# Gated mix of a feature-map linear attention and a GeGLU network: the attention state accumulated transposed, with v as the stationary operand, and turned by DMA

## The chip, the cores and the metric

The kernel runs on one core of one Trainium2 chip. A time is in device microseconds (us) of one execution, and the times that are compared are medians of several runs. The kernel before takes 303.22 us (three runs, 303.22 to 305.41). The profile is of one execution; its span, 301.2 us, is a little shorter than the time of that run (302.93 us), because it does not hold everything that the time holds.

The engines are named as in the profile: PE multiplies matrices and has a part PEld that loads the stationary operand; DVE works elementwise and reduces; ACT applies functions and copies; POOL is a third elementwise engine; SP issues most of the DMA transfers. PE's results go to PSUM, which the kernel uses as eight banks of 512 float32 per partition.

## What is computed

One token block of 2048 rows and 640 columns, `x`, goes through two branches. Branch A is linear attention with 32 heads of 20 columns; branch B is a gated network of width 1728. A gate per row mixes them. Cut to what matters:

```python
qkv = (x @ wqkv).reshape(B, S, 3, H, Dh).transpose(2, 0, 3, 1, 4)   # H = 32, Dh = 20
pq = einsum("bhsd,hdf->bhsf", q, w_phi)                  # and pk from k
phi_q = concat([softmax(pq), softmax(-pq)])              # over the 20 features of a head
phi_k = concat([softmax(pk), softmax(-pk)])
kv = einsum("bhsf,bhsd->bhfd", phi_k, v)                 # the state: summed over all rows
z  = einsum("bhsf->bhf", phi_k)
o  = einsum("bhqf,bhfd->bhqd", phi_q, kv) / (einsum("bhqf,bhf->bhq", phi_q, z)[..., None] + 1e-6)
a  = o.reshape(B, S, D) @ wo
b  = (gelu(x @ w_gate) * (x @ w_up)) @ w_down
g  = sigmoid((x * gate_w).sum(-1, keepdims=True))
out = g * a + (1 - g) * b
```

The state `kv` with `z` as one more column is needed whole before the first row of `o` can be computed.

## The kernel before

The 2048 rows are 16 tiles of 128. `wk2` and `wq2` are the key and query weights with `w_phi` multiplied in; the kernel makes them itself, in ten *folds* (five for k, five for q, one for each 128 rows of the weights). `xT` is x with its columns on the partitions; block 0 (tiles 0 to 3) is turned on PE, and blocks 1 to 3 come turned by DMA. The loads that the change touches, in the order of SP's queue:

```python
        wload(self.wkT, D, "wkT")      # transposing DMA of the key weights, for the k folds
        xblock(1)                      # transposing DMA: xT of tiles 4 to 7
        wload(self.wqT, 0, "wqT")
        xblock(2)
        xblock(3)
        ...                            # then the weights of branch B and wo
```

The first stage in program order. `vs` and `ve` are v of tiles 0 to 3; `f(kt, which, banks, engine)` is a fold of six matmuls with 640 columns in all, copied out of PSUM by DVE ("d") or ACT ("a"):

```python
        f = self.fold
        f(0, "k", (6, 7), "d")
        f(1, "k", (0, 1), "a")
        self.v_early(4, 2)             # v of tile 4: 5 matmuls of 512 columns, 5 of 128; copied out by ACT
        f(2, "k", (4, 5), "d")
        f(3, "k", (6, 7), "d")
        self.v_early(5, 0)
        f(4, "k", (4, 5), "d")
        self.k_early(0, 2)             # pk of tile 0: 5 matmuls of 384, 5 of 257; ACT takes exp twice (Ek), then gcol
        f(0, "q", (6, 7), "d")
        f(1, "q", (4, 5), "d")
        self.k_early(1, 0)
        f(2, "q", (6, 7), "d")
        f(3, "q", (4, 5), "d")
        self.k_norm(0)                 # softmax sums and division of Ek on DVE
        self.k_early(2, 2)
        f(4, "q", (6, 7), "a")
        self.k_norm(1)
        self.k_early(3, 0)
        self.pq(0, 1, 1)               # exp(pq), exp(-pq) of 4 tiles x 128 features: 5 matmuls of 512, bank 6 + n % 2
        self.pq(0, 0, 0)
        self.pq(0, 3, 3)
        self.gram(0)
        self.k_norm(2)
        self.pq(0, 2, 2)
        self.k_norm(3)
        n = 4
        g = 1
        for t in range(4, NT):
            if t < 6:
                self.k_early(t, 1)
            else:
                self.vk(t)             # v and pk of one tile: 15 matmuls, 1281 columns x 5
            self.k_norm(t)
            m = 4 + ((t - 3) * (len(order) - 4) + 11) // 12
            while n < m:               # one or two pq for each tile, the grams before the last of them
                ...
```

The gram of a tile adds its part to the state. The keys' features, 128 at a time, are the stationary operand, and v with a column of ones for each head (`vaug`, 21 columns a head) streams past. Only the heads that share a chunk of 128 features are streamed; twelve matmuls, 1512 columns in all, fill banks 3, 4 and 5:

```python
        return {
            3: [full(0, 0), full(0, 1), full(0, 3), (1, 2, 12, 14)],
            4: [full(1, 0), full(1, 1), full(1, 3), (1, 2, 15, 17)],
            5: [full(0, 4), full(1, 4), full(0, 2), (1, 2, 18, 19)],
        }
        ...
                    self.bank(b)[:, c:c + n], self.Ek[:, se, s, i * P:(i + 1) * P], self.vaug[:, sv, h0:h1 + 1, :],
```

After the last tile `kv_evac` multiplies the state by a mask that keeps each head's own block and writes it to `KV` in bfloat16, twelve operations of DVE. `num(t)` then has `KV` streamed past exp(pq): twelve matmuls of 1584 columns, followed by DVE, POOL and a transposing DMA.

Branch B, `ffn`, is interleaved with the end of it. `gateup(b, c)` is ten matmuls of 512 columns, one ACT and one DVE operation (five matmuls for the narrow chunk 13); `down(t)` multiplies by `w_down` and `wo` (38 matmuls of 320 columns):

```python
            if b == 0:
                order = [0, 1, 13] + list(range(2, 13))
                at = {5: 0, 8: 1, 11: 2}          # after which gateup num(0), num(1), num(2) follow
            ...
                if b == 0:
                    if idx == 0:
                        self.gram(14)
                    if idx == 3:
                        self.gram(15)
                        self.kv_evac()
                        self.gates()
                if idx in at:
                    self.num(at[idx])
```

Of the kernel before, what the change touches and what calls it, by code (L numbers as in the profile page):

```python
# [3 lines left out]
P = 128  # L4
# [99 lines left out]
class _Kernel:  # L104
# [99 lines left out]
    def loads(self):  # L204
# [23 lines left out]
        def xblock(b):  # L228
            sc.dma("sp", lambda e: e.dma_start_transpose(
                self.xT[:, :, b * self.BT:(b + 1) * self.BT], self.x[b * self.BT:(b + 1) * self.BT, :]),  # L230
                writes=[("xT", t) for t in range(b * 4, b * 4 + 4)])
        wload(self.wkT, D, "wkT")
        xblock(1)
        wload(self.wqT, 0, "wqT")
        xblock(2)
        xblock(3)
# [133 lines left out]
                start=(kt == 0 and col == 0), stop=(kt == self.KD - 1), skip_group_check=True),  # L370
                reads=[("xT", t), ("wv", kt)], writes=[("ps", bk)], signal=(kt == self.KD - 1))

    def k_step(self, t, kt):
        sc = self.sc
        for c0, n, bk, col in ((640, 384, 2 * t, 128), (1024, 257, 2 * t + 1, 0)):
            sc.op("pe", lambda e, c0=c0, n=n, bk=bk, col=col: e.matmul(
                self.bank(bk)[:, col:col + n], self.xT[:, kt, t * P:(t + 1) * P], self.w3[:, kt, c0:c0 + n],
                start=(kt == 0), stop=(kt == self.KD - 1)),
                reads=[("xT", t), ("wk2", kt), "wgate"], writes=[("ps", bk)], signal=(kt == self.KD - 1))

    def v_first_evac(self, ts, ek, tail):
        sv, nt = ts[0], len(ts)
        h0, nh = (24, 8) if tail else (0, 24)
# [62 lines left out]
            sc.op("dve", lambda e, v=v, r=r: e.tensor_tensor(v, v, r, ALU.mult),  # L446
                  reads=[("Rk", se)], writes=[("Ek", se, s)])

    def gram_regions(self):
        lo = self.HLO  # L450
        full = lambda s, i: (s, i, lo[i], self.HHI[i])
        return {
            3: [full(0, 0), full(0, 1), full(0, 3), (1, 2, 12, 14)],
            4: [full(1, 0), full(1, 1), full(1, 3), (1, 2, 15, 17)],
            5: [full(0, 4), full(1, 4), full(0, 2), (1, 2, 18, 19)],
        }

    def gram(self, t):
        sc = self.sc
        se, sv = t % self.NSE, t % self.NSV  # L460
        for b, regs in self.gram_regions().items():
            c = 0
            for r, (s, i, h0, h1) in enumerate(regs):
                n = (h1 - h0 + 1) * self.DA
                sc.op("pe", lambda e, s=s, i=i, h0=h0, h1=h1, c=c, n=n, b=b, r=r: e.matmul(  # L465
                    self.bank(b)[:, c:c + n], self.Ek[:, se, s, i * P:(i + 1) * P], self.vaug[:, sv, h0:h1 + 1, :],
                    start=(t == 0 and r == 0), stop=(t == self.NT - 1 and r == len(regs) - 1)),
                    reads=[("Ek", se, s), ("vaug", sv), ("vmain", sv), ("vone", sv)], writes=[("ps", b)],
                    signal=(r == len(regs) - 1))
                c += n  # L470

    def kv_evac(self):
        sc = self.sc
        for b, regs in self.gram_regions().items():
            c = 0
            for (s, i, h0, h1) in regs:
                nh = h1 - h0 + 1
                j0 = h0 - self.HLO[i]
                dst = self.KV[:, i, s, j0 * self.DB:(j0 + nh) * self.DB].rearrange(
                    "p (h c) -> p h c", c=self.DB)[:, :, 0:self.DA]  # L480
                src = self.bank(b)[:, c:c + nh * self.DA].rearrange("p (h c) -> p h c", c=self.DA)
                m = self.mask[:, i, j0:j0 + nh].unsqueeze(2).to_broadcast([P, nh, self.DA])
                sc.op("dve", lambda e, dst=dst, src=src, m=m: e.tensor_tensor(dst, src, m, ALU.mult),
                      reads=[("ps", b), ("mask", i), ("KVd", i, s)], writes=[("KV", i, s, h0)])
                c += nh * self.DA

    def pq(self, b, i, n):
        sc = self.sc
# [22 lines left out]
    def attention_state(self):  # L511
        NT = self.NT
        order = [(b, i) for b in range(self.NB) for i in range(self.KD)]
        sc = self.sc
        sc.op("dve", lambda e: e.memset(self.zero[:, :], 0.0), writes=["zero"])
        sc.op("dve", lambda e: e.memset(self.one[:, :], 1.0), writes=["one"])

        def warm(n):
            for i in range(n):
                sc.op("pe", lambda e: e.matmul(self.bank(0), self.zero[:, 0:P], self.zero[:, :], start=True, stop=True),  # L520
                      reads=["zero"], writes=[("ps", 0)])
        vs, ve, xt = self.v_step, self.v_first_evac, self.x_transpose
# [24 lines left out]
        ks = self.k_step  # L547
        f = self.fold
        f(0, "k", (6, 7), "d")
        f(1, "k", (0, 1), "a")  # L550
        self.v_early(4, 2)
        f(2, "k", (4, 5), "d")
        f(3, "k", (6, 7), "d")
        self.v_early(5, 0)
        f(4, "k", (4, 5), "d")
        self.k_early(0, 2)
        f(0, "q", (6, 7), "d")
        f(1, "q", (4, 5), "d")
        self.k_early(1, 0)
        f(2, "q", (6, 7), "d")  # L560
        f(3, "q", (4, 5), "d")
        self.k_norm(0)
        self.k_early(2, 2)
        f(4, "q", (6, 7), "a")
        self.k_norm(1)
        self.k_early(3, 0)
        self.pq(0, 1, 1)
        self.pq(0, 0, 0)
        self.pq(0, 3, 3)
# [4 lines that stand above are left out]
        n = 4  # L574
        g = 1
        for t in range(4, NT):
            if t < 6:
                self.k_early(t, 1)
            else:
                self.vk(t)  # L580
            self.k_norm(t)
            m = 4 + ((t - 3) * (len(order) - 4) + 11) // 12
            while n < m:
                if n == m - 1:
                    for g in range(g, t - 2 if t < 8 else t - 1):
# [36 lines left out]
    def num(self, t):  # L622
# [5 lines left out]
        kvk = {(i, s): [] for i in range(5) for s in (0, 1)}  # L628
        for regs in self.gram_regions().values():
            for (s, i, h0, h1) in regs:  # L630
                kvk[(i, s)].append(("KV", i, s, h0))
        for hf in (0, 1):
            for s in (0, 1):
                bk = NBK + 2 * hf + s
                for r, (i, h0, h1) in enumerate(parts[hf]):
                    n = (h1 - h0 + 1) * DB
                    o0 = (h0 - 16 * hf) * DB
                    k0 = (h0 - self.HLO[i]) * DB
                    sc.op("pe", lambda e, s=s, i=i, n=n, o0=o0, k0=k0, bk=bk, r=r: e.matmul(  # L639
                        self.bank(bk)[:, o0:o0 + n], self.Eq[:, s, i, t * P:(t + 1) * P],  # L640
                        self.KV[:, i, s, k0:k0 + n], start=(r == 0), stop=(r == 2), skip_group_check=True),
                        reads=[("Eq", t // 4, s, i), ("KVd", i, s)] + kvk[(i, s)], writes=[("ps", bk)],
                        signal=(r == 2))
        sl = t % 2
        N = self.ps[:, NBK * 512:(NBK + 4) * 512].rearrange("p (f s c) -> p f s c", s=2, c=512)[:, :, :, 0:16 * DB]
# [76 lines left out]
    def ffn(self):  # L722
# [4 lines left out]
        for b in range(self.NB):  # L727
            if b == 0:
                order = [0, 1, 13] + list(range(2, 13))
                at = {5: 0, 8: 1, 11: 2}  # L730
            else:
                order = list(range(14))
                at = {2: 4 * b + 1, 6: 4 * b + 2, 10: 4 * b + 3}
            for idx, c in enumerate(order):
                if b == 0 and c == 13:
                    self.gateup(b, c, (2,))
                else:
                    self.gateup(b, c, pairs[self.pn % 2])
                    self.pn += 1
# [4 lines that stand above are left out]
                        self.gram(15)  # L744
                        self.kv_evac()
                        self.gates()
                if idx in at:
                    self.num(at[idx])
            for t in range(4):
# [48 lines left out]
```

The softmax here doesn't subtract the row's maximum and nothing guards it: scores larger than these inputs give would overflow.

## Time and profile before

The stages of the one execution, read from the trace in order of time (us from the start of the span), with the busy time of PE, DVE and ACT in it:

| stretch | what runs | PE | DVE | ACT |
|---|---|---|---|---|
| 0 to 10 | loads, turning of block 0, first v | 8.71 | 1.30 | 2.58 |
| 10 to 30 | last v of tiles 0 to 3, folds, first pk, first pq | 18.26 | 15.59 | 12.80 |
| 30 to 60 | tile by tile: v, pk, gram, pq | 29.76 | 27.46 | 20.31 |
| 60 to 301 | rest of that loop, then branch B with the nums | 237.35 | 117.03 | 67.77 |

A busy time of PE counts each matmul from its start to its modelled end, and neighbours overlap, so a stretch in which PE is 98% busy can still have gaps between the starts of its matmuls. What PE waited for is read from the idle entries of its groups and from the chain of work that ended last, and the length of a piece of work from the start of one group to the start of the next.

### The profile page before, as it was taken

Reading aid. Unit: us, or ns where it says so; the run is one execution under the profiler, and the core shown is the slowest. Engines: PE = TensorE matmul, PEld = TensorE weight load, DVE = VectorE, ACT = ScalarE, POOL = GpSimd, SP = SyncE. Lnnn points to the kernel's source line nnn. Section 1 sums busy time; section 2 is a strip of 40 time slices with the busy share of each in tenths; the row PEclk is TensorE's granted clock in tenths of the full one; section 3 lists DMA queues with packets and bytes.
Section 4 is the critical chain, followed back from the end, with each engine's and each line's share of the span. In section 5 each row is a group of like instructions: output and inputs, shape, how many; then the busy total and the mean of one; then the engine's idle time right before and its main releaser. Section 6 shows DMA issues by size and latency. Waiting matters only on the chain.

```text
span 301.2 us, 4951 instructions
## 1 busy us (share of the span) xinstructions
PE 294.1 (98%) x1973; PEld 173.9 (58%) x1999; DVE 161.4 (54%) x317; ACT 103.5 (34%) x182; POOL 29.0 (10%) x58
## 2 busy tenths in 40 slices
PE   8998999999999999999999999999999999999996
PEld 4665656555554555776454577655457765445773
DVE  1469999768685877214467700445770045567000
ACT  3358767576773222112222211222221122222112
POOL 7000000000000022011011100101110010111000
PEclk9999999999999999999999999999999999999999
DMA  7999980000000011110111010011101011110101
GB/s 221 248 214 337 372 285 0 0 2 0 2 0 0 2 22 24 46 44 25 43 25 22 0 46 22 27 41 23 24 0 44 24 33 32 25 22 0 46 22 44
DMA packets 35474, 18.11 MB, mean 60 GB/s; under 512 B 27579, under 2 KB 35196, under 8 KB 35452
## 3 DMA queue, kind: packets, MB, share of 16 engines
q1 hardware_dynamic: 34800, 17.78, 21.8%
q8 instruction: 15, 0.25, 0.4%
q10 hardware_dynamic: 652, 0.03, 0.2%
q14 instruction: 7, 0.06, 0.1%
HBM read 8.96 MB, written 2.62 MB: 38 GB/s over the span
## 4 chain that ended last, share of the span: by engine, by line
PE 92%; SPq 2%; DMA 2%; ACT 1%; issue 1%; DVE 0%; DVEq 0%; ACTq 0%
PE ps L602 36%; PE ps L684 20%; PE ps L359 12%; PE ps L690 7%; PE ps L491 7%; PE ps L639 4%; PE ps L465 4%; DMA xT<-in_A_x_dram 2%; PE ps L612 1%; SPq L226 1%; SPq L216 1%; PE ps L339 1%; ACT Eq L497 1%; ACT Ek L426 0%; DVE w_49 L352 0%
## 5 line engine op out<-in xcount | busy, mean ns | idle before, releaser
L602 PE MATMUL ps<-xT,wu_sb 128*128 128x512 bf16 x253 | 64.2, 379 | 0.8 <-ACT Eq L497 0.2
L684 PE MATMUL ps<-wd_sb,hT 128*128 128x320 bf16 (+2 forms) x447 | 63.5, 299 | 0.1
L602 PE MATMUL ps<-xT,wg_sb 128*128 128x512 bf16 x252 | 63.0, 379 | 0.2
L605 ACT ACTIVATE gl<-ps 128x512 bf16<-128x512 f32 x52 | 31.0, 597 | 83.3 <-PE ps L602 74.2
L607 DVE TENSOR_TENSOR hT<-ps,gl 128x512 bf16<-128x512 f32 x52 | 35.7, 688 | 42.9 <-PE ps L602 42.9
L684 PEld LDWEIGHTS ps<-wd_sb,hT 128*128 128x128 bf16 x448 | 43.1, 98 | 18.2 <-DVE hT L607 0.4
L602 PEld LDWEIGHTS ps<-xT,wu_sb 128*128 128x128 bf16 x260 | 25.4, 98 | 31.1 <-issue 0.7
L359 PE MATMUL ps<-w_49,xT 128*128 128x512 bf16 (+3 forms) x226 | 40.7, 327 | 1.1 <-DMA xT<-in_A_x_dram 0.6
L602 PEld LDWEIGHTS ps<-xT,wg_sb 128*128 128x128 bf16 x260 | 24.9, 98 | 26.9
L668 POOL TENSOR_TENSOR Og<-O_57,O_58 128x640 bf16<-128x640 bf16 x16 | 22.3, 1394 | 167.9 <-DVE O_58 L666 167.9
L700 ACT ACTIVATE outsb<-ps,Gm 128x640 bf16<-128x640 f32 (+2 forms) x17 | 13.0, 762 | 74.1 <-PE ps L690 74.1
L359 PEld LDWEIGHTS ps<-w_49,xT 128*128 128x128 bf16 x230 | 21.7, 97 | 19.7 <-DVE w_49 L352 0.7
L655 DVE RECIPROCAL RH<-ps 128x32 f32<-128x32 f32 x16 | 5.7, 358 | 43.9 <-PE ps L639 42.8
L437 DVE TENSOR_REDUCE Dk<-Ek 128x64 f32<-128x1280 bf16 x16 | 23.7, 1482 | 8.9 <-ACT gcol L429 8.9
L446 DVE TENSOR_TENSOR Ek<-Ek,Dk 128x640 bf16<-128x640 bf16 x32 | 25.0, 822 | 0.6
L690 PE MATMUL ps<-wo_sb,goT 128*128 128x320 bf16 (+2 forms) x160 | 24.5, 299 | 0.0
L491 PE MATMUL ps<-xT,wq_50 128*128 128x512 bf16 x94 | 23.4, 378 | 1.1 <-ACT wq_50 L354 0.7
L497 ACT ACTIVATE Eq<-ps 128x512 bf16<-128x512 f32 x40 | 21.8, 603 | 5.7 <-PE ps L491 5.6
L426 ACT ACTIVATE Ek<-ps 128x640 bf16<-128x640 f32 x32 | 20.8, 706 | 3.4 <-PE ps L359 3.4
L690 PEld LDWEIGHTS ps<-wo_sb,goT 128*128 128x128 bf16 x160 | 15.5, 98 | 6.3
L639 PEld LDWEIGHTS ps<-KV,Eq 128*128 128x128 bf16 x192 | 12.0, 98 | 3.1
L491 PEld LDWEIGHTS ps<-xT,wq_50 128*128 128x128 bf16 x100 | 8.6, 97 | 8.8 <-ACT wq_50 L354 0.7
(66 smaller groups left out, 175.9 us busy)
## 6 DMA issues: line engine op xcount, KB each, us to landing
out_dram<-outsb SPq DMA_DIRECT2D x15, 160.0 KB, 1.8
wd_sb<-in_B_w_down_dram SPq DMA_DIRECT2D x1, 2080.0 KB, 13.5
wg_sb<-in_B_w_gate_dram SPq DMA_DIRECT2D x1, 1120.0 KB, 5.8
wu_sb<-in_B_w_up_dram SPq DMA_DIRECT2D x1, 1120.0 KB, 8.2
wg_sb<-in_B_w_gate_dram SPq DMA_DIRECT2D x1, 960.0 KB, 9.6
wu_sb<-in_B_w_up_dram SPq DMA_DIRECT2D x1, 960.0 KB, 10.4
w_49<-in_A_wqkv_dram SPq DMA_DIRECT2D x5, 160.0 KB, 4.0
wo_sb<-in_A_wo_dram SPq DMA_DIRECT2D x1, 800.0 KB, 10.2
```

The source lines that it names most:

```text
L359: sc.op("pe", lambda e, kt=kt: e.matmul(self.bank(bank)[:, bcol:bcol + n], self.xT[:, kt, t * P:(t + 1) * P], self.w3[:, kt, c0:c0 + n], s ...
L437: sc.op("dve", lambda e: e.tensor_reduce(self.Dk[:, se, 0, :].rearrange("p (s h) -> p s h", h=H), self.Ek[:, se, :, :].rearrange("p s (h d ...
L446: sc.op("dve", lambda e, v=v, r=r: e.tensor_tensor(v, v, r, ALU.mult), reads=[("Rk", se)], writes=[("Ek", se, s)])
L491: sc.op("pe", lambda e, kt=kt: e.matmul(self.bank(bank), self.wq2[:, kt, i * P:(i + 1) * P], self.xT[:, kt, b * self.BT:(b + 1) * self.BT] ...
L497: sc.op("act", lambda e, s=s, scale=scale: e.activation(self.Eq[:, s, i, b * self.BT:(b + 1) * self.BT], self.bank(bank), AF.Exp, scale=sc ...
L602: sc.op("pe", lambda e, kt=kt, w=w, bk=bk: e.matmul(self.bank(bk), w[:, kt, c * P:(c + 1) * P], xs(kt), start=(kt == 0), stop=(kt == self. ...
L605: sc.op("act", lambda e: e.activation(self.gl[:, slot, :], self.bank(banks[0]), AF.Gelu_apprx_tanh), reads=[("ps", banks[0])], writes=[("g ...
L607: sc.op("dve", lambda e: e.tensor_tensor(self.hT[:, c, :], self.bank(banks[1]), self.gl[:, slot, :], ALU.mult), reads=[("ps", banks[1]), ( ...
L639: sc.op("pe", lambda e, s=s, i=i, n=n, o0=o0, k0=k0, bk=bk, r=r: e.matmul(self.bank(bk)[:, o0:o0 + n], self.Eq[:, s, i, t * P:(t + 1) * P] ...
L668: sc.op("pool", lambda e: e.tensor_tensor(self.Og[:, sl, :], self.O1[:, sl, :], self.O2[:, sl, :], ALU.add), reads=[("O", 0, sl), ("O", 1, ...
L684: sc.op("pe", lambda e: e.matmul(self.bank(bk, w), self.hT[:, c, tt * P:(tt + 1) * P], self.wd_sb[:, c, w0:w0 + w], start=(c == 0), stop=F ...
L690: sc.op("pe", lambda e: e.matmul(self.bank(bk, w), self.goT[:, gs, k, :], self.wo_sb[:, k, w0:w0 + w], start=False, stop=(k == self.KD - 1 ...
```

## The change

Four things are changed.

1. *The gram has v stationary and the keys stream.* Six groups of six heads (the last has two). For a group the stationary operand is 128 columns of `vaug` (six heads are 126), and the streamed one is the group's 120 features of both signs, 240 columns; the last group has 80. It makes the state transposed: v on the partitions, features along the free axis. Six matmuls, 1280 columns, instead of twelve and 1512.
2. *The state is turned by DMA.* `kv_evac` copies the three banks into two slots of `Ek` that are free by then (three copies on DVE, one on ACT), and two transposing DMAs turn them into two other slots. Ten masking operations on DVE, now a step of their own (`kv_mask`) after the gateup at position 6, write `KV`. The first three nums move from after positions 5, 8 and 11 to after 8, 11 and 13.
3. *v of tiles 4 to 7 runs early, in between the k folds*, two of them ahead of the first fold; the loop's tiles 6 and 7 then need only pk, and the pq are spread so that tiles 4 to 7 have two each. The banks of the folds change, and the last q fold is copied by DVE instead of ACT.
4. *The second block of x is loaded ahead of the key weights*, so that v of tiles 4 and 5 can start before the key weights are there.

The diff, cut to its core (an unused function is removed as well):

```diff
+        xblock(1)
         wload(self.wkT, D, "wkT")
-        xblock(1)
         wload(self.wqT, 0, "wqT")
@@ gram
-    def gram_regions(self): ...
+    def gram_groups(self):
+        fe = 6 * self.DH
+        for g in range(6):
+            lo = min(6 * g * self.DA, self.H * self.DA - P)
+            yield g, 3 + g % 2 if g < 4 else 5, 2 * fe * (g // 2 if g < 4 else g - 4), lo, fe * g, min(fe, self.D - fe * g)
...
+        for g, b, c, lo, f0, nf in self.gram_groups():
+            sc.op("pe", lambda e: e.matmul(
+                self.bank(b)[:, c:c + 2 * nf], va[:, lo:lo + P], self.Ek[:, se, :, f0:f0 + nf],
+                start=(t == 0 and g in (0, 1, 4)), stop=(t == self.NT - 1 and g in (2, 3, 5)), skip_group_check=True),
@@ kv_evac: copies of banks 3 (DVE), 4 (ACT), 5 (DVE, twice) into Ek slots 0 and 1, then
+        for pl in (0, 1):
+            sc.dma("sp", lambda e: e.dma_start_transpose(
+                self.Ek[:, 2 + pl, :, :].rearrange("p s (i c) -> p (s i) c", c=P),
+                self.Ek[:, pl, :, :].rearrange("p s f -> p (s f)")), ...)
+    def kv_mask(self):
...
+                sc.op("dve", lambda e: e.tensor_tensor(dst, src, m, ALU.mult), ...)      # ten of them
@@ attention_state
-        f(0, "k", (6, 7), "d")
-        f(1, "k", (0, 1), "a")
-        self.v_early(4, 2)
-        f(2, "k", (4, 5), "d")
-        f(3, "k", (6, 7), "d")
+        self.v_early(4, 6)
         self.v_early(5, 0)
-        f(4, "k", (4, 5), "d")
+        f(0, "k", (2, 3), "d")
+        f(1, "k", (4, 5), "a")
+        self.v_early(6, 6)
+        f(2, "k", (2, 3), "d")
+        f(3, "k", (4, 5), "a")
+        f(4, "k", (0, 1), "d")
+        self.v_early(7, 6)
         self.k_early(0, 2)
-        f(0, "q", (6, 7), "d")
-        f(1, "q", (4, 5), "d")
+        f(0, "q", (4, 5), "d")
+        f(1, "q", (6, 7), "d")
         self.k_early(1, 0)
-        f(2, "q", (6, 7), "d")
-        f(3, "q", (4, 5), "d")
+        f(2, "q", (4, 5), "d")
+        f(3, "q", (6, 7), "d")
+        self.k_early(2, 2)
+        f(4, "q", (4, 5), "d")
         self.k_norm(0)
-        self.k_early(2, 2)
-        f(4, "q", (6, 7), "a")
+        self.k_early(3, 0)
         self.k_norm(1)
-        self.k_early(3, 0)
         self.pq(0, 1, 1)
...
-            if t < 6:
+            if t < 8:
                 self.k_early(t, 1)
...
-            m = 4 + ((t - 3) * (len(order) - 4) + 11) // 12
+            m = 2 * t - 2 if t < 8 else t + 5
@@ ffn
-                at = {5: 0, 8: 1, 11: 2}
+                at = {8: 0, 11: 1, 13: 2}
...
+                    if idx == 6:
+                        self.kv_mask()
```

More of the change, by code (lines that the diff above doesn't have):

```diff
@@ L371, in v_step @@
                 reads=[("xT", t), ("wv", kt)], writes=[("ps", bk)], signal=(kt == self.KD - 1))
[L373 to L379, printed above, removed]
     def v_first_evac(self, ts, ek, tail):
@@ L447, in k_norm @@
                   reads=[("Rk", se)], writes=[("Ek", se, s)])
[L449 to L456, printed above, removed]
+    def gram_groups(self):
[3 more added lines that the diff above has]
+            yield g, 3 + g % 2 if g < 4 else 5, 2 * fe * (g // 2 if g < 4 else g - 4), lo, fe * g, min(fe, self.D - fe * g)
     def gram(self, t):
@@ L460, in gram @@
         se, sv = t % self.NSE, t % self.NSV
[L461 to L470, printed above, removed]
+        va = self.vaug[:, sv, :, :].rearrange("p h c -> p (h c)")
@@ L472, in kv_evac @@
+        for g, b, c, lo, f0, nf in self.gram_groups():
+            sc.op("pe", lambda e: e.matmul(
+                self.bank(b)[:, c:c + 2 * nf], va[:, lo:lo + P], self.Ek[:, se, :, f0:f0 + nf],
+                start=(t == 0 and g in (0, 1, 4)), stop=(t == self.NT - 1 and g in (2, 3, 5)), skip_group_check=True),
+                reads=[("Ek", se, 0), ("Ek", se, 1), ("vaug", sv), ("vmain", sv), ("vone", sv)], writes=[("ps", b)],
+                signal=(g in (2, 3, 5)))
     def kv_evac(self):
@@ L473, in kv_evac @@
         sc = self.sc
[L474 to L485, printed above, removed]
+        fe = 6 * self.DH
@@ new lines, in copy @@
+        def copy(ek, dst, src, rd, wr):
+            if ek == "d":
+                sc.op("dve", lambda e: e.tensor_copy(dst, src), reads=rd, writes=wr)
+            else:
+                sc.op("act", lambda e: e.activation(dst, src, AF.Copy), reads=rd, writes=wr)
+        for pl, ek in ((0, "d"), (1, "a")):
+            f = pl * fe
+            dst = self.Ek[:, pl, :, 0:4 * fe].rearrange("p s (b c) -> p b s c", c=2 * fe)[:, :, :, f:f + fe]
+            src = self.bank(3 + pl, 4 * fe).rearrange("p (b s f) -> p b s f", f=fe, s=2)
+            copy(ek, dst, src, [("ps", 3 + pl)], [("Ek", pl, 0)])
@@ new lines, in kv_evac @@
+        for pl, ek in ((0, "d"), (1, "d")):
+            g = 4 + pl
+            nf = min(fe, self.D - fe * g)
+            src = self.bank(5)[:, pl * 2 * fe:pl * 2 * fe + 2 * nf].rearrange("p (s f) -> p s f", f=nf)
+            copy(ek, self.Ek[:, pl, :, fe * g:fe * g + nf], src, [("ps", 5)], [("Ek", pl, 1)])
+        for pl in (0, 1):
+            sc.dma("sp", lambda e: e.dma_start_transpose(
+                self.Ek[:, 2 + pl, :, :].rearrange("p s (i c) -> p (s i) c", c=P),
+                self.Ek[:, pl, :, :].rearrange("p s f -> p (s f)")),
+                reads=[("Ek", pl, 0), ("Ek", pl, 1)], writes=[("Ek", 2 + pl, 0), ("Ek", 2 + pl, 1)])
@@ new lines, in kv_mask @@
+    def kv_mask(self):
+        sc = self.sc
+        self.kvk = {i: [] for i in range(self.KD)}
+        lows = {g: lo for g, b, c, lo, f0, nf in self.gram_groups()}
+        for i in range(self.KD):
+            for g in range(self.HLO[i] // 6, self.HHI[i] // 6 + 1):
+                h0, h1 = max(self.HLO[i], 6 * g), min(self.HHI[i], 6 * g + 5)
+                nh, j0 = h1 - h0 + 1, h0 - self.HLO[i]
+                o = i * P + h0 * self.DA - lows[g]
+                dst = self.KV[:, i, :, j0 * self.DB:(j0 + nh) * self.DB].rearrange(
+                    "p s (h c) -> p s h c", c=self.DB)[:, :, :, 0:self.DA]
+                src = self.Ek[:, 2 + g % 2, :, o:o + nh * self.DA].rearrange("p s (h c) -> p s h c", c=self.DA)
+                m = self.mask[:, i, j0:j0 + nh].unsqueeze(1).unsqueeze(3).to_broadcast([P, 2, nh, self.DA])
+                sc.op("dve", lambda e: e.tensor_tensor(dst, src, m, ALU.mult),
+                      reads=[("Ek", 2 + g % 2, 0), ("mask", i), ("KVd", i, 0), ("KVd", i, 1)], writes=[("KV", i, g)])
+                self.kvk[i].append(("KV", i, g))
@@ L546, in attention_state @@
         ve([3], "d", True)
-        ks = self.k_step
         f = self.fold
-        f(0, "k", (6, 7), "d")
-        f(1, "k", (0, 1), "a")
-        self.v_early(4, 2)
-        f(2, "k", (4, 5), "d")
-        f(3, "k", (6, 7), "d")
-        self.v_early(5, 0)
-        f(4, "k", (4, 5), "d")
+        self.v_early(4, 6)
+        self.v_early(5, 0)
+        f(0, "k", (2, 3), "d")
[5 more added lines that the diff above has]
+        self.v_early(7, 6)
         self.k_early(0, 2)
-        f(0, "q", (6, 7), "d")
-        f(1, "q", (4, 5), "d")
+        f(0, "q", (4, 5), "d")
+        f(1, "q", (6, 7), "d")
         self.k_early(1, 0)
-        f(2, "q", (6, 7), "d")
-        f(3, "q", (4, 5), "d")
+        f(2, "q", (4, 5), "d")
+        f(3, "q", (6, 7), "d")
+        self.k_early(2, 2)
+        f(4, "q", (4, 5), "d")
         self.k_norm(0)
-        self.k_early(2, 2)
-        f(4, "q", (6, 7), "a")
+        self.k_early(3, 0)
         self.k_norm(1)
-        self.k_early(3, 0)
         self.pq(0, 1, 1)
@@ L627, in num @@
         parts = {0: [(0, 0, 6), (1, 6, 12), (2, 12, 15)], 1: [(2, 16, 19), (3, 19, 25), (4, 25, 31)]}
[L628 to L631, printed above, removed]
         for hf in (0, 1):
@@ L641, in num @@
                         self.KV[:, i, s, k0:k0 + n], start=(r == 0), stop=(r == 2), skip_group_check=True),
-                        reads=[("Eq", t // 4, s, i), ("KVd", i, s)] + kvk[(i, s)], writes=[("ps", bk)],
+                        reads=[("Eq", t // 4, s, i), ("KVd", i, s)] + self.kvk[i], writes=[("ps", bk)],
                         signal=(r == 2))
```

## The prediction

> **What bounds the kernel now.** I began with the page: the busy shares, then the engines in the chain of work that ended last.
>
> ```profile
> PE 294.1 (98%) x1973; PEld 173.9 (58%) x1999; DVE 161.4 (54%) x317; ACT 103.5 (34%) x182; POOL 29.0 (10%) x58
> ...
> PE 92%; SPq 2%; DMA 2%; ACT 1%; issue 1%; DVE 0%; DVEq 0%; ACTq 0%
> ```
>
> PE is the bound nearly everywhere, so only two things can shorten the time: fewer columns through PE, or fewer moments in which PE waits. What a column costs I read from the chain in order of time (start, length, line), where pieces of one kind stand back to back:
>
> ```profile
> 50.76 1.35 PE ps L465 x24
> 52.11 1.08 PE ps L491 x5
> 53.19 2.71 PE ps L359 x15
> ...
> 95.85 4.32 PE ps L602 x20
> 100.17 0.70 PE ps L639 x12
> ```
>
> Each piece starts where the one before ends. A matmul of 512 columns takes 4.32 / 20 = 0.216 us; one gram is 1.35 / 2 = 0.675 us for 1512 columns; one tile's v and pk is 2.71 us; one pq is 1.08 us. Is there idle time in the tile loop? From pk of tile 4 (30.72) to the end of the last pq (86.62) are 55.90 us. Its contents: two pk at 1.36, ten v with pk at 2.71, sixteen pq at 1.083, thirteen grams at 0.675: 2.72 + 27.1 + 17.33 + 8.78 = 55.93. So the loop has no idle time at all; there only columns count.
>
> The waits lie earlier. This is PE's own timeline (start, length with the modelled end, line, shapes; the idle entry in brackets):
>
> ```profile
> 12.27 0.79 PE L339 MATMUL ps<-BD,wkT 128*128 128x140 bf16 x12
> 13.71 1.31 PE L359 MATMUL ps<-w_49,xT 128*128 128x512 bf16 x9 [0.65 <-DMA xT<-in_A_x_dram]
> ...
> 17.15 0.81 PE L359 MATMUL ps<-w_49,xT 128*128 128x384 bf16 x4
> 18.30 0.89 PE L359 MATMUL ps<-w_49,xT 128*128 128x384 bf16 x6 [0.34 <-DVE w_49 L352]
> ...
> 23.32 1.53 PE L359 MATMUL ps<-w_49,xT 128*128 128x384 bf16 x10
> 25.51 3.46 PE L491 MATMUL ps<-xT,wq_50 128*128 128x512 bf16 x14 [0.66 <-ACT wq_50 L354]
> ```
>
> Three waits: v of tile 4 for the second x block, pk of tile 0 for DVE's copy of the last k fold, the first pq for ACT's copy of the last q fold. I count the stall as a whole: from 12.27 to 30.72 are 18.45 us, and the work in it is ten folds (0.63 a pair, 3.2 us), two v and four pk at 1.36 (8.15), four pq (4.33), one gram (0.675), together 16.3. Stall: 2.1 us. Behind the loop the first gateup waits about 0.15 us for the last exp, which stays.
>
> [...] The rows of the old gram's weight loads are 97 ns long, yet twelve matmuls follow each other every 56 ns, so the loads overlap. [...]
>
> **Part 1, the gram.** 1280 columns in six matmuls: [...] 0.127 us less, sixteen times, 2.03 us. All of it is on PE's path. In the loop nothing else may become the bound: tiles 8 to 15 then take 2.71 + 0.55 + 1.08 = 4.34 us each, tiles 4 to 7 take 1.36 + 2 x 1.08 + 0.55 = 4.07; DVE's softmax work for a tile is 1.48 + 0.58 + 1.56 = 3.6 us; ACT's is at most 0.71 + 1.36 + 1.1 = 3.2, or 1.36 + 2.2 = 3.6 with two pq. The tightest point is gram 6 in the turn of tile 8: DVE, busy without a break from the last q copy on (which I put at 25.9), has tile 6 normalised at 25.9 + 7 x 3.6 = 51.1, and PE gets there at about 51.4.
>
> **Parts 3 and 4, the early stage.** In the page's DMA part (median us from issue to landing at the end):
>
> ```profile
> xT<-in_A_x_dram SPq DMA_TRANSPOSE x3, 5.1
> ...
> wkT<-in_A_wqkv_dram SPq DMA_TRANSPOSE x1, 6.3
> wqT<-in_A_wqkv_dram SPq DMA_TRANSPOSE x1, 6.8
> ```
>
> The second x block is now issued at 4.18, where wkT was, and lands at about 9.3, ahead of 12.25 where v of tile 4 starts: its wait goes. wkT is issued at about 7.1 and should land where the second of the two landed before, at about 13.4; the first fold comes after two v, at 12.25 + 2.72 = 14.97: 1.5 us of room. The k folds then have v of tiles 6 and 7 between them, so copies are done in time (the last k copy ends about 19.1, pk of tile 0 starts about 19.4), and the last q copy has the whole pk of tile 3 to finish: the second and third waits go as well. One stays and grows: the third pq needs bank 7, which ACT frees only after its exps of tile 3 (0.25 after pk of tile 3 ends, 1.37 long) and the two exps of the first pq (1.09): 2.8 us after pk of tile 3, while PE gets there after two pq, 2.17. That leaves 0.6 us, where 0.26 was lost at this place before. v of tile 7 may lose another 0.1 on its bank. Stall 0.7 instead of 2.1: 1.4 us gained. Pulling v of tiles 6 and 7 ahead moves 2.7 us of PE work and neither adds nor removes any.
>
> **Part 2, the turn of the state.** What is after gram 15 is off PE's path if it is done by the new place of num(0). Take G for the end of gram 15. DVE's copies (about 0.65, 0.35 and 0.2 us, estimates from the old masking rows and the 0.82 us for 640 columns in L352) end near G + 1.4. The page has 2.6 us from issue to landing for a turned output of five 128 x 128 pieces, each 1.2 us of SP:
>
> ```profile
> goT<-Og SPq DMA_TRANSPOSE x16, 2.6
> ```
>
> These have ten pieces; between 1.2 us of issue for five and 2.9 for twenty I take 2.0, and 3.6 to landing, so the second lands near G + 1.3 + 2.0 + 3.6 = G + 6.9. Masking comes in DVE's order after the hT of position 6, at G + 7.4. Ten operations with 1512 elements per partition are about 2.5 us (the old twelve took 2.43), so KV is there at G + 9.9; num(0) follows position 8 at G + 10.8. Room: 0.9 us. hT of position 7 is late by about 1 us, but its bank is not wanted before G + 11.5. The first three nums come two or three gateups later than before; a num needs some 3.6 us of DVE, 1.4 of POOL and 2.6 of DMA, and by that num(2) and num(3) are still 6 us or more ahead of the down that uses them. Cost on the path: none.
>
> **The sum.** 2.03 + 1.4 = 3.4 us. 303.22 - 3.4 = 299.8 us; the span becomes about 297.8.
>
> **Rivals.** *The weight load becomes the gram's bound.* The slices of v start at columns 126, 252, 378, 504 and 544, not at multiples of 128 as the slices of Ek did, and the streamed operand is now in two runs of 120. If either slowed the array, [...] the gain of 2.0 falls away, about 301.8; doubled, 305. Against it: loads overlap everywhere in this trace, and v with its 21-column grid was streamed at full rate.
>
> *The state comes late.* DVE works in order, so if the DMAs land 2 us later than I think, every hT behind the masks waits, then PE waits for banks: 1 to 3 us, 301 to 303. For it: the room is only 0.5 us at the masks. Against it: with nothing else in the DMA queues then, the old 2.6 us is steady.
>
> *The early waits only change their names.* wkT behind the x block may land after 15, or the exps of pk on ACT hold more pq than I saw. Then the 1.4 us shrink to nothing: 301.2.
>
> **Range and chances.** All three rivals leave at most small losses, and they can hardly come together. More gain than 4.1 us, all stall and the gram's, is not in sight. I give 298.6 to 301.6. 2% is 6 us, more than PE could save: faster 0.03, same 0.94, slower 0.03.
>
> **What would show each step right or wrong.** The gram's pieces in the chain: 0.55 us for six. In PE's timeline, no wait for xT or the copied folds before the first pq, and about 0.6 us at the third pq for Eq. The two transposing DMAs of Ek: about 2.0 us of issue, landing before the first mask. First num behind position 8 without idle time of PE. If the time falls by under 2 us, the gram's pieces tell whether the array or a wait took it; if it falls by over 5, I have missed idle time that no view here showed.

## The result, and the profile after

| | time, us | runs | ratio to before, 95% interval |
|---|---|---|---|
| before | 303.49 | 303.22 to 305.41 | |
| changed | 299.60 | 299.51 to 300.02 | 0.9861 [0.9819, 0.9903] |
| changed, measured again with the last experiments | 299.67 | 299.56 to 299.95 | 0.9881 [0.9865, 0.9898] |

The change saves 3.5 to 3.9 us of the time; the spans of the two profiled runs, 301.2 and 297.8 us, differ by 3.4. The page of the changed kernel still has PE busy 98% of the span, but its share of the chain has gone from 92% to 96%. Most of that is the first stage: before, the chain ran through SP's issues and the second x block until v of tile 4 started at 13.71; now it runs through PE from 5.45 on.

```profile
PE 292.9 (98%) x1913; PEld 171.9 (58%) x1913; DVE 162.2 (54%) x318; ACT 104.3 (35%) x183; POOL 29.0 (10%) x58
...
PE 96%; DMA 1%; ACT 1%; issue 0%; SPq 0%; ACTq 0%
```

In the views below, hT is the product that DVE makes of a gateup, Eq the exps of a pq and Ek those of a pk, both made by ACT, and KV the masked state. The chain in order of time (start, length, line; L452 is the gram, L504 a pq, L359 v and pk, L616 a gateup, L649 a num):

```profile
50.92 1.10 PE ps L452 x12
52.02 1.08 PE ps L504 x5
53.10 2.71 PE ps L359 x15
...
92.45 10.79 PE ps L616 x50
103.24 0.69 PE ps L649 x12
```

Two grams take 1.10 us, where they took 1.35. The fifty matmuls from 92.45 on are the five gateups between gram 15 and the first num: 50 x 0.216 = 10.79, so the turn of the state, which happens beside them, holds PE up nowhere.

PE's own timeline of the early stage:

```profile
12.10 2.88 PE L359 MATMUL ps<-w,xT 128*128 128x512 bf16 x20
14.99 0.80 PE L339 MATMUL ps<-BD,wkT 128*128 128x140 bf16 x12
...
25.04 1.53 PE L359 MATMUL ps<-w,xT 128*128 128x384 bf16 x10
26.40 2.32 PE L504 MATMUL ps<-xT,wq 128*128 128x512 bf16 x10
29.06 1.25 PE L504 MATMUL ps<-xT,wq 128*128 128x512 bf16 x5 [0.34 <-ACT Eq L510]
30.15 0.71 PE L452 MATMUL ps<-Ek,vaug 128*128 128x240 bf16 x6
...
31.77 1.52 PE L359 MATMUL ps<-w,xT 128*128 128x384 bf16 x10
```

v of tile 4 starts when the v before it ends; pk of tile 3 (25.04) runs into the first pq without a gap. Two waits are left in this stage. The first fold starts at 14.99 though two v from 12.10 end at 12.10 + 2.72 = 14.82: 0.17 us for the key weights. The third pq starts at 29.06, though two pq from 26.40 end at 28.56: 0.50 us. The two make 0.67 us. The prediction counted 2.1 us of stall before, with its start, 12.27, from PE's timeline and its end, 30.72, from the chain, where a piece begins at the modelled end of the one before, 0.16 us later. PE's timeline of the kernel before has that pk of tile 4 earlier:

```profile
30.56 1.53 PE L359 MATMUL ps<-w_49,xT 128*128 128x384 bf16 x10
```

From 12.27 to 30.56 are 18.29 us for 16.36 of work: the stall was 1.9 us. The changed kernel, counted in the same way, takes 19.67 us from 12.10 to 31.77 for 18.96 of work (v of tiles 6 and 7 is now among it): 0.7 us. So 1.2 us were gained here. PE also reached this stage 0.17 us earlier, at 12.10; that moment lies between 11.9 and 13.0 in the traces of this study.

SP's queue at the start of the changed kernel:

```profile
4.19 3.83 SPq L229 DMA_TRANSPOSE xT<-in_A_x_dram  x1
8.06 3.35 SPq L226 DMA_TRANSPOSE wkT<-in_A_wqkv_dram  x1
```

The turn of the state, from the timeline of ACT, DVE, SP and PE (gram 15 ends at 92.45):

```profile
92.34 0.57 ACT L466 ACTIVATE Ek<-ps 128x480 bf16<-128x480 f32 x1 [0.89 <-PE ps L452]
92.54 1.11 DVE L464 CAST Ek<-ps 128x480 bf16<-128x480 f32 x3
...
93.66 2.85 SPq L478 DMA_TRANSPOSE Ek<-Ek  x2
...
98.96 0.69 DVE L621 TENSOR_TENSOR hT<-ps,gl 128x512 bf16<-128x512 f32 x1 [1.47 <-PE ps L616]
99.57 2.34 DVE L496 TENSOR_TENSOR KV<-Ek,mask 128x252 bf16<-128x252 bf16 x10
...
103.08 0.85 PE L649 MATMUL ps<-KV,Eq 128*128 128x154 bf16 x12
```

And the DMA part, with the us from issue to landing at the end of the line:

```profile
Ek<-Ek SPq DMA_TRANSPOSE x2, 3.4
wkT<-in_A_wqkv_dram SPq DMA_TRANSPOSE x1, 6.9
```

The second transposing DMA is issued at about 95.2 and lands at about 98.6. The masks start at 99.57, straight behind the hT of position 6 and without waiting, and end at 101.91, 1.2 us before the first num.

### The profile page after: what moved, and what is told of

It is laid out like the page before. It is cut to its first block, busy times and chain, and to the rows that moved or that the text cites. A ratio compares the mean times of both kernels' runs of the same rounds, so it can differ in the third digit from the quotient of the medians.

```text
span 297.8 us, 4821 instructions
## 1 busy us (share of the span) xinstructions
PE 292.9 (98%) x1913; PEld 171.9 (58%) x1913; DVE 162.2 (54%) x318; ACT 104.3 (35%) x183; POOL 29.0 (10%) x58
## 4 chain that ended last, share of the span: by engine, by line
PE 96%; DMA 1%; ACT 1%; issue 0%; SPq 0%; ACTq 0%
PE ps L616 37%; PE ps L694 20%; PE ps L359 13%; PE ps L700 7%; PE ps L504 7%; PE ps L649 4%; PE ps L452 3%; PE ps L368 2%; PE ps L626 1%; DMA xtok<-in_A_x_dram 1%; PE ps L339 1%; ACT Eq L510 1%; ACT Ek L418 0%; PE ps L284 0%; PE ps L304 0%
## 5 line engine op out<-in xcount | busy, mean ns | idle before, releaser
L616 PE MATMUL ps<-xT,wu_sb 128*128 128x512 bf16 x260 | 64.6, 379 | 0.2 <-ACT Eq L510 0.2
L616 PE MATMUL ps<-xT,wg_sb 128*128 128x512 bf16 x260 | 64.6, 379 | 0.0
L616 PEld LDWEIGHTS ps<-xT,wu_sb 128*128 128x128 bf16 x260 | 25.4, 98 | 31.1 <-issue 0.7
L359 PE MATMUL ps<-w,xT 128*128 128x512 bf16 (+3 forms) x240 | 40.9, 321 | 0.0
L616 PEld LDWEIGHTS ps<-xT,wg_sb 128*128 128x128 bf16 x260 | 25.0, 98 | 27.2
L678 POOL TENSOR_TENSOR Og<-O,O 128x640 bf16<-128x640 bf16 x16 | 22.3, 1394 | 167.5 <-DVE O L676 167.5
L359 PEld LDWEIGHTS ps<-w,xT 128*128 128x128 bf16 x240 | 22.4, 97 | 18.2
L504 PE MATMUL ps<-xT,wq 128*128 128x512 bf16 x100 | 24.7, 379 | 0.3 <-ACT Eq L510 0.3
L676 DVE TENSOR_TENSOR O<-ps,RH 128x640 bf16<-128x640 f32 x32 | 24.8, 816 | 0.0
L649 PEld LDWEIGHTS ps<-KV,Eq 128*128 128x128 bf16 x192 | 12.0, 98 | 3.1
```

Source lines behind the costliest of these rows:

```text
L359: sc.op("pe", lambda e, kt=kt: e.matmul(self.bank(bank)[:, bcol:bcol + n], self.xT[:, kt, t * P:(t + 1) * P], self.w3[:, kt, c0:c0 + n], s ...
L504: sc.op("pe", lambda e, kt=kt: e.matmul(self.bank(bank), self.wq2[:, kt, i * P:(i + 1) * P], self.xT[:, kt, b * self.BT:(b + 1) * self.BT] ...
L616: sc.op("pe", lambda e, kt=kt, w=w, bk=bk: e.matmul(self.bank(bk), w[:, kt, c * P:(c + 1) * P], xs(kt), start=(kt == 0), stop=(kt == self. ...
L676: dve(lambda e, o=o, f=f, s=s: e.tensor_tensor(o, V[s][:, :, :, 0:DH], f, ALU.mult), rb + [key(6 + s)], [("O", s, sl)], guard=old)
```

## The experiments

Each run was compared with the kernel before on the same chip; those runs had medians of 303.28, 303.13, 303.18 and 303.11 us in the four groups below. The changed kernel itself ran again in one group only; elsewhere a difference from it is one from its 299.60 us. The intervals are 0.4 to 0.7 us wide to each side, so what is smaller than that is read from the traces.

### One half of the change at a time

*The gram and the turn alone.* The load order, the order of v and folds and the spread of the pq are put back:

```diff
-        xblock(1)
         wload(self.wkT, D, "wkT")
+        xblock(1)
-        self.v_early(4, 6)  ...            # the whole early order of the changed kernel
+        f(0, "k", (6, 7), "d")  ...        # the whole early order of the kernel before
-            if t < 8:
+            if t < 6:
-            m = 2 * t - 2 if t < 8 else t + 5
+            m = 4 + ((t - 3) * (len(order) - 4) + 11) // 12
```

> The new gram and the turn by DMA, with the early stage (order of v and folds, loads, spread of the pq) as in the kernel before. My theory: the gram saves 16 x 0.127 = 2.0 us of PE and the turn costs nothing on the path, so 303.5 - 2.0 = 301.5 us, and the old waits for the x block, the k copy and the q copy are all still there. Rival (the turn of the state costs something that the early stage pays for): 302 or more, with PE idle between gram 15 and the second num. Rival (all of the gain is the early stage): 303.5.

Measured: 301.33 us, ratio 0.9930 [0.9917, 0.9944], so 1.95 us less than before. The old waits are in PE's timeline of this run, the first of them shorter than before (0.65 us there), and its chain has the fifty matmuls before the first num (L614 is a gateup here) at 10.79 us too:

```profile
13.13 1.53 PE L359 MATMUL ps<-w,xT 128*128 128x512 bf16 x10 [0.20 <-DMA xT<-in_A_x_dram]
...
17.96 0.89 PE L359 MATMUL ps<-w,xT 128*128 128x384 bf16 x6 [0.34 <-DVE w L352]
...
24.94 3.68 PE L504 MATMUL ps<-xT,wq 128*128 128x512 bf16 x15 [0.43 <-ACT wq L354]
```

```profile
93.45 10.79 PE ps L614 x50
```

The gram is worth what was predicted for it, 2.0 us, and the turn is free.

*The early stage alone.* The reverse: the early order, the loads and the spread of the changed kernel with the old gram, `kv_evac` and places of the nums.

> The early stage of the changed kernel (order, loads, spread of the pq) with the gram and the state of the kernel before. My theory: the early stall of 2.1 us shrinks to about 0.7, so 303.5 - 1.4 = 302.1 us, and with the run of the gram alone it adds up to the whole gain. Rival (the early stage is worth nothing without the shorter gram, since the spread of the pq loads ACT and DVE more): 303.5.

Measured: 301.93 us, ratio 0.9958 [0.9945, 0.9971]: 1.35 us less. The third pq starts at 29.13 after pq that end at 28.63, the same 0.5 us wait:

```profile
29.13 1.25 PE L491 MATMUL ps<-xT,wq 128*128 128x512 bf16 x5 [0.34 <-ACT Eq L497]
```

The two halves add up: 1.95 + 1.35 = 3.3, and 0.9930 x 0.9958 = 0.9888, beside 0.9881 for the whole in the second measurement. Neither half needs the other.

*The order of the two loads.* The changed kernel with the key weights first again:

```diff
-        xblock(1)
         wload(self.wkT, D, "wkT")
+        xblock(1)
```

> The changed kernel with the key weights loaded ahead of the second x block again, as before. My theory: v of tile 4 is ready to start at 12.1 and waits for x until about 13.4, the first fold no longer waits 0.17 us for the key weights; about 1.2 us lost, 300.8 us. Rival (the reordering of the loads is hidden and only the order of PE's work counts): 299.6.

Measured: 301.01 us (eight executions, 300.70 to 303.88), ratio 0.9935 [0.9912, 0.9959], 1.4 us more than the changed kernel. PE's timeline of this run:

```profile
13.47 2.89 PE L359 MATMUL ps<-w,xT 128*128 128x512 bf16 x20 [1.11 <-DMA xT<-in_A_x_dram]
16.20 0.79 PE L339 MATMUL ps<-BD,wkT 128*128 128x140 bf16 x12
```

v of tile 4 waits for the x block until 13.47, and the fold follows v without a wait. Without the swap of the loads, the new order of PE's work loses nearly all that the early stage gains.

### How much room the turn of the state has

*The masks at once,* behind the copies, instead of behind the gateup at position 6:

```diff
                         self.kv_evac()
+                        self.kv_mask()
                         self.gates()
-                    if idx == 6:
-                        self.kv_mask()
```

> The changed kernel with the masking steps right behind the copies of the state, the nums where they are. My theory: DVE waits in its order for both transposing DMAs (landing near 98.6), masks until 100.9, then does the gate columns and the hT of position 4 until about 102.5, while PE wants that hT's bank at 97.7: about 4.8 us lost, 304.4 us. Rival (PE has enough buffered banks to ride over it): 299.6 to 300.

Measured: 306.74 us, ratio 1.0109 [1.0096, 1.0122], slower than the kernel before by 1.1% and than the changed one by 7.1 us. The mechanism is the expected one, but it costs more. DVE and PE in this run:

```profile
97.85 0.42 DVE L496 TENSOR_TENSOR KV<-Ek,mask 128x252 bf16<-128x252 bf16 x1 [3.49 <-DMA Ek<-Ek]
...
99.32 2.03 DVE L496 TENSOR_TENSOR KV<-Ek,mask 128x42 bf16<-128x42 bf16 x9 [1.05 <-DMA Ek<-Ek]
...
102.00 1.22 DVE L621 TENSOR_TENSOR hT<-ps,gl 128x512 bf16<-128x512 f32 x2
102.69 2.20 PE L616 MATMUL ps<-xT,wu_sb 128*128 128x512 bf16 x5 [4.14 <-DVE hT L621]
...
106.54 1.24 PE L616 MATMUL ps<-xT,wu_sb 128*128 128x512 bf16 x5
```

DVE waits 3.49 and 1.05 us for the two DMAs; the hT behind the masks comes at 102.0, and PE stands idle for 4.14 us. Then ten matmuls take from 102.69 to 106.54, 3.85 us, where ten take 2.16 earlier in this run (87.21 to 89.37). The table by stretches says why (its columns: the stretch and its length, busy time with the number of instructions of PE, PEld, DVE, ACT and POOL, then the granted clock, the DMA share and GB/s):

```profile
100.00:103.00 3.00, 0.31 (x2) 0.14 (x3) 2.93 (x12) 0.00 (x0) 0.00 (x0) 0.97 0.00 0
103.00:106.00 3.00, 3.00 (x9) 1.04 (x8) 0.92 (x2) 0.00 (x0) 0.00 (x0) 0.50 0.00 0
```

The granted clock is 0.50 from 103 to 106, behind the 4.14 us without a matmul; from 84 to 100 it was 1.00, and from 106 to 110 it is 0.97. What sets it was not shown. The wait is thus worth 4.3 us (102.69 instead of 98.4 in this run) and the clock 1.7 more. The remaining 0.7 of the 6.7 us between the spans arose before the first fold of this run (15.71 instead of 14.99). The other three executions took 306.56 to 306.91 us, at a mean granted clock of 0.989 against 0.994 in this one; no trace shows how the clock ran in them.

*The masks one gateup earlier* than in the changed kernel (`idx == 5` instead of `idx == 6`):

> The changed kernel with the masks one gateup earlier, after position 5. My theory: DVE waits in its order from about 97.5 to 98.6 for the second DMA, masks until 100.9 and does the hT of position 6 until 101.6, while PE wants that bank at about 102.0: nothing lost, 299.6 us. Rival (any wait of DVE for the DMA reaches PE): 300.6 or more.

Measured: 300.06 us (299.30 to 300.92), ratio 0.9898 [0.9880, 0.9915]. That lies between the two expectations and does not decide; the trace does. Its span is 297.7 us, the changed kernel's 297.8. DVE waits 0.81 us for the second DMA, and in the chain PE's fifty matmuls still take 10.79 us:

```profile
98.56 2.03 DVE L496 TENSOR_TENSOR KV<-Ek,mask 128x42 bf16<-128x42 bf16 x9 [0.81 <-DMA Ek<-Ek]
```

```profile
92.38 10.79 PE ps L616 x50
```

The hT of positions 6 and 7 are done at 101.78, and the wait of 0.81 us, which ended before PE wanted the banks behind it, cost PE nothing.

*The first num one gateup earlier* (`at = {7: 0, 11: 1, 13: 2}`):

> The changed kernel with the first num after position 7 instead of 8, the masks where they are. My theory: PE is there at 100.9, the last mask ends at 101.9 and only the last four matmuls of the num need it, so about 0.6 us are lost, 300.2 us. Rival (the turn has far more room than I think): 299.6. Rival (the num holds DVE's hT behind it as well): 301 or more.

Measured: 300.28 us, ratio 0.9902 [0.9888, 0.9916], 0.6 us over the changed kernel; span 298.3 against 297.8. DVE, PEld and PE in this run:

```profile
99.39 2.35 DVE L496 TENSOR_TENSOR KV<-Ek,mask 128x252 bf16<-128x252 bf16 x10
...
101.88 0.40 PE L649 MATMUL ps<-KV,Eq 128*128 128x154 bf16 x4 [0.21 <-DVE KV L496]
```

The num begins at 100.73 and waits for masks on its way, longest before its last four matmuls, which need the last one: they end at about 102.1 instead of 101.4. So of the two places tried, the changed kernel's, one gateup later, is the one that is free.

### The waits that are left

*The third pq in another bank,* since only bank 7 held it:

```diff
-        bank = 6 + n % 2
+        bank = 2 if n == 3 else 6 + n % 2
```

> The changed kernel with the third pq written to bank 2 instead of bank 7 (bank 2 is free from the end of the exps of tile 2 until the pk of tile 4). My theory: the 0.5 us that PE loses before the third pq goes, since only the bank held it: 299.6 - 0.5 = 299.1 us. Rival (ACT is behind with its exps, so the wait moves to the fourth pq or to the pk of tile 4): 299.6.

Measured: 299.89 us, ratio 0.9889 [0.9874, 0.9903]: nothing gained. PE's timeline of this run:

```profile
26.27 3.40 PE L504 MATMUL ps<-xT,wq 128*128 128x512 bf16 x15
29.68 0.71 PE L452 MATMUL ps<-Ek,vaug 128*128 128x240 bf16 x6
...
50.29 0.71 PE L452 MATMUL ps<-Ek,vaug 128*128 128x240 bf16 x6
51.16 0.71 PE L452 MATMUL ps<-Ek,vaug 128*128 128x240 bf16 x6 [0.15 <-DVE Ek L438]
```

The wait at the third pq is gone: fifteen matmuls follow each other from 26.27 on and end at 29.52. But gram 0 starts only at 29.68, behind DVE, which finishes tile 0 at 29.58, and gram 6 starts at 51.16 though gram 5 ends at 50.84. That is 0.16 + 0.32 us, all of the 0.5. My rival was wrong about the place (neither the fourth pq nor a pk waits) and right about the outcome; the engine that took the gain is DVE, not ACT. From the last q copy to 54 us DVE works on softmax without a break, 3.58 us for each tile, and its tile 6 is done at 51.06.

*The first gateup on banks 0 and 1 as well* (`pairs = [(0, 1), (6, 7)]`, beside the third pq in bank 2), where nothing waits for the last exp:

> The same as the run before, and the gateups start with banks 0 and 1 instead of 6 and 7, so that the first of them does not wait for the last exp of the pq. My theory: another 0.15 us, 298.95 us. Rival (the first gateups are held by ACT's table load anyway): as the run before, 299.1.

Measured: 299.50 us, ratio 0.9874 [0.9860, 0.9889], 0.4 us under the run before, with an interval that overlaps. The first gateup, its two halves in the changed kernel and then in this run:

```profile
83.29 1.24 PE L616 MATMUL ps<-xT,wg_sb 128*128 128x512 bf16 x5
84.72 1.24 PE L616 MATMUL ps<-xT,wu_sb 128*128 128x512 bf16 x5 [0.19 <-ACT Eq L510]
```

```profile
83.63 1.24 PE L616 MATMUL ps<-xT,wg_sb 128*128 128x512 bf16 x5
...
84.71 1.24 PE L616 MATMUL ps<-xT,wu_sb 128*128 128x512 bf16 x5
```

The wait is gone, and it was longer than 0.15 us. Five matmuls take 1.08 us from start to start. In the changed kernel the second five start 1.43 us after the first, so 0.35 us were lost, about what the times differ by; here they start 1.08 us after, though ACT's table load takes 1.28 us in this run (from 84.93) as in the changed kernel (from 84.59), so the rival of the table load falls. The entry in brackets is smaller because it counts from the modelled end of the matmul before, 0.16 us behind the start that the next one could have had; the same is true of the 0.34 at the third pq, where 0.50 was lost.

*Those two grams later,* with both changes of banks kept: gram 0 behind the fourth pq, which gets bank 0, and gram 6 in the turn of tile 9:

```diff
-        bank = 2 if n == 3 else 6 + n % 2
+        bank = {2: 0, 3: 2}.get(n, 6 + n % 2)
-        self.gram(0)
         self.k_norm(2)
         self.pq(0, 2, 2)
+        self.gram(0)
-                    for g in range(g, t - 2 if t < 8 else t - 1):
+                    for g in range(g, t - 2 if t < 9 else t - 1):
...                                        # the same for the line that sets g behind the loop
-        pairs = [(6, 7), (0, 1)]
+        pairs = [(0, 1), (6, 7)]
```

> The run with both bank changes, and the two grams that waited for DVE's softmax work come later: gram 0 behind the fourth pq (which gets bank 0), gram 6 in the turn of tile 9. My theory: the 0.5 us at the third pq came back as 0.16 us before gram 0 and 0.3 us before gram 6, because DVE is busy without a break from 26 to 54; with both grams moved PE keeps the whole gain, 0.65 us under the changed kernel of this call. Rival (DVE then holds later grams instead, so nothing is kept): 0.15 us under it.

Measured: 299.26 us (298.77 to 299.70), ratio 0.9868 [0.9852, 0.9885], 0.4 us under the changed kernel of the same group (299.67 us, 299.56 to 299.95) where 0.65 was expected; the ranges overlap. That kernel's expectation was:

> The changed kernel once more, unaltered, as the measure for the run beside it: 299.6 us.

In the trace no gram waits for DVE any more, and the 0.50 us at the third pq and the 0.35 at the first gateup are gone. But the profiled run, the slowest of its four at 299.70 us, shows another loss:

```profile
15.93 0.80 PE L339 MATMUL ps<-BD,wkT 128*128 128x140 bf16 x12 [1.00 <-DMA wkT<-in_A_wqkv_dram]
```

The key weights land at 15.9 in this run, 1.16 us after the two v ahead of the fold could have ended; in the changed kernel beside it the fold is 0.52 us late. In the eight traces of kernels with this load order in which the landing was read, the key weights land between about 14.6 and 15.9; in six of all eleven traces with this order the first fold waits for them, 0.2 to 1.2 us.

*Three v ahead of the first fold,* so that it comes at about 16, then three k folds together, and two q folds before the first pk:

```diff
         self.v_early(4, 6)
         self.v_early(5, 0)
+        self.v_early(6, 6)
         f(0, "k", (2, 3), "d")
         f(1, "k", (4, 5), "a")
-        self.v_early(6, 6)
-        f(2, "k", (2, 3), "d")
-        f(3, "k", (4, 5), "a")
-        f(4, "k", (0, 1), "d")
+        f(2, "k", (0, 1), "d")
         self.v_early(7, 6)
-        self.k_early(0, 2)
-        f(0, "q", (4, 5), "d")
+        f(3, "k", (2, 3), "d")
+        f(4, "k", (4, 5), "a")
+        f(0, "q", (0, 1), "d")
         f(1, "q", (6, 7), "d")
+        self.k_early(0, 2)
         ...                                # pk and q folds go on; f(4, "q") and k_norm(0) before pk of tile 2
```

> The run with the later grams, and v of tiles 4, 5 and 6 all ahead of the first k fold, three k folds in a row, and the first two q folds ahead of the first pk. My theory: the key weights land at 14.9 to 15.9, not at 13.4, so that the first fold waits 0.2 to 1 us; with three v in front it starts at 16.2 and waits for nothing: 0.2 to 0.5 us under the run with the later grams of this call. Rival (the wait only moves on to the q folds, whose weights are now wanted 1.6 us earlier, at 19.1): no gain.

Measured: 298.73 us (298.57 to 299.41), ratio 0.9863 [0.9847, 0.9880], span 296.8; beside it the run with the later grams at 299.12 us (298.79 to 299.31), 0.4 us more, though the ranges overlap. Its expectation was:

> The run with the later grams once more, unaltered, as the measure for the run beside it: 299.3 us.

PE's timeline of the run with three v first:

```profile
11.88 4.24 PE L359 MATMUL ps<-w,xT 128*128 128x512 bf16 x30
15.96 1.11 PE L339 MATMUL ps<-BD,wkT 128*128 128x140 bf16 x18
...
18.97 0.87 PE L339 MATMUL ps<-BD,wqT 128*128 128x140 bf16 x12
19.81 1.54 PE L359 MATMUL ps<-w,xT 128*128 128x384 bf16 x10
...
26.22 4.48 PE L504 MATMUL ps<-xT,wq 128*128 128x512 bf16 x20
30.53 0.71 PE L452 MATMUL ps<-Ek,vaug 128*128 128x240 bf16 x6
```

The first fold no longer waits, where 0.6 us were lost in the run with the later grams, and neither do the q folds: they start at 18.97, 0.63 us after the pair of k folds before them. One small loss is left. From the pair of q folds at 18.97 to pk of tile 0 at 19.81 are 0.84 us instead of 0.63. That pk wants the bank of a k fold that DVE copies; that it was held by this copy is my estimate. This run is the fastest version of this study, 0.9 us under the changed kernel by the medians of two groups (298.73 and 299.67); their intervals against the kernel before overlap, while their runs do not. The traces bear it out: the changed kernel lost 0.17 + 0.50 + 0.35 us, this one 0.2.

## Why the prediction was right, step by step

**The time.** 299.8 us were predicted and 299.60 measured; the span was put at 297.8 and is 297.8. Both terms of the sum stand on their own in the two half changes. That it fits to the tenth is luck: the sum started from 303.22, where the result has 303.49 for the kernel before, and in the spans the stall gave 1.2 us instead of 1.4, while PE happened to reach the early stage 0.17 us earlier.

**The gram: right.** 0.55 us for one instead of 0.675. What was put on record, 0.127 us less for each, was my estimate. Two pieces of the chain before give the same as an estimate: 0.216 us for a matmul of 512 columns and 0.70 for twelve of 132 come to 0.415 ns a column and 3.5 ns a matmul, so 0.55 us for six with 1280 columns. The rival that the odd starts of the slices of v, or the streamed operand in two runs, would slow the array falls: six matmuls take 0.55 us in the chain of every run with the new gram whose chain was read at a gram, ten of them.

**The early stage: right in sum, wrong in one term.** The stall is 0.7 us, as predicted, but not from the terms I gave, and before it was 1.9, not 2.1. "wkT is issued at about 7.1 and should land ... at about 13.4 ...: 1.5 us of room" is the step that failed. It was issued at 8.06, since the x block ahead of it took 3.83 us of issue time, not 2.9, and landed 6.9 us later at about 15.0, after the fold could have started. I had taken the landing of the second of the two loads from a trace in which that was the smaller one, and the x block's 2.9 us from one in which it came second: in second place it took 2.90 us of issue time in the trace of the kernel before, in first place 3.3 to 4.7 in eight traces. The term cost 0.17 us in the profiled run, 0.2 to 1.2 in five others, and nothing in five. At the third pq 0.6 us were predicted (the terms given, 0.25 + 1.37 + 1.09, make 2.71 and so 0.54) and 0.50 came; v of tile 7 lost nothing where I had put 0.1. That these misses nearly cancel is luck too. The rival that the early waits only change their names was right in kind, with about an eighth of the 1.4 us I gave it in the profiled run. Behind the loop the first gateup lost 0.35 us rather than 0.15, in both kernels.

**The turn of the state: right, with a little more room.** Ten pieces cost SP 1.34 us, not 2.0, and 3.4 us to landing, not 3.6; the masks took 2.34, not 2.5. So the masks are done 9.5 us after gram 15, not 9.9, and the first num starts 10.8 after it, as computed. The rival of a late state falls for this placing; the run with the masks at once shows that it is the placing that makes it fall.

**The tight point at gram 6: right.** It was put at 51.1 for DVE against 51.4 for PE. In the changed kernel DVE finishes tile 6 at 51.17 and gram 6 starts at about 51.3. That is why removing the 0.5 us before it brought nothing at first.

## What to carry to other kernels

Where PE is the bound, count the streamed columns: here 1280 instead of 1512 made a gram 0.55 us long instead of 0.675, and the run with that alone was 1.95 us faster, although the result has to be turned. The turn cost nothing where its consumer stands behind the landing (98.6, the masks at 99.57). With the masks placed at once, DVE waited 3.49 and 1.05 us, the hT behind them in its order were late, and the run was 7.1 us slower than the changed kernel: the place of the waiting step in the program is part of the cost. And when a wait is taken away, look at once for the engine with the next smallest room, here DVE with 0.1 us.

## What the runs showed that I had not expected

In one run an idle time of PE came with more loss than its length: with the masks at once, 4.14 us without a matmul were followed by about 3 us at a granted clock of 0.50, and the loss was 6.0 us instead of 4.3. And the landing of one load, the key weights, moved by over 1 us between runs of kernels with the same loads (14.6 to 15.9 in eight traces). Most of that comes from the x block ahead of it, which took 3.3 to 4.7 us of issue time; the time from issue to landing moved only from 6.9 to 7.5. Why the issue time varies was not tried.
